# Experts' weight loads: the float64 half piece queued ahead of the step's float32 piece

## The chip, the core and the metric

One core of a Trainium2 chip runs the kernel. The metric is the device time of one execution in microseconds (us). Five engines matter: TensorE (PE, matrix products and transposes; its weight loads are PEld), VectorE (DVE), ScalarE (ACT), GpSimd (POOL) and SyncE (SP), which only starts transfers. Each engine works through its own instructions in order and waits at semaphores for the others. A transfer started by SP, ACT or POOL is carried out by 16 DMA engines beside them.

## What is computed

Three layers follow one another on 1536 tokens of width 512: attention with local and global keys, a mixture of 8 experts of which each token takes 2, and a last dense layer.

```python
x = attention(q, k, v)                      # 2 x 768 tokens, 8 heads of 64
logits = x @ w_gate + log1p(exp(x @ w_noise)) * noise
top2, top2_w = two_largest(logits)          # softmax weights of the two
for e in range(8):                          # tokens that chose expert e
    h = maximum(x[mask] @ w1[e], 0)         # 512 -> 1024
    out[mask] += top2_w[mask] * (h @ w2[e]) # 1024 -> 512
h = out @ w_in                              # 512 -> 2048
y = (h * tanh(softplus(h))) @ w_out         # 2048 -> 512
```

The weights of the experts come as float32, those of the last layer as float64.

## The kernel before

The program has three stages: attention (to about 124 us), the experts (to about 464 us) and the last layer. Every product is made of three: a float32 number is split into a rounded part, `hi`, and the rest, `lo`, and PE adds hi x hi, hi x lo and lo x hi (`three`, L767 to L769).

The experts' stage is a loop over 64 steps. Step n = 8e + f is expert e, slice f. In each step the program writes down, and every engine keeps that order for itself:

- `first_layer(n)`: 12 products into `hp`, then ACT makes `hhi` (L813) and DVE `hlo` (L814);
- in slices 2 to 4 `turn_out`: four transposes of the last expert's result into the one PSUM tile `tq`, a copy to `ys` by ACT (L849), and a store to `yd` on ACT's queue (L850);
- `whole_layer(n - 1)`: 12 products into the four tiles `ac`, with the `hhi` and `hlo` of the step before;
- in slices 3 to 6 of experts 1 to 6 `turn_in`: four transposes (L801) of the next expert's tokens `xg` into the same `tq`, split by ACT (L772) and DVE (L773);
- `w_split`: the float32 piece n + 2 of the experts' weights (128 x 1024, in a tile `raw`) is split, `whi` by ACT (L264) and `wlo` by DVE (L267);
- `w_load`: SP starts the load of piece n + 4 (L252, 512 KB);
- in slices 1, 3 and 5 (in the first expert 3, 5 and 7, at the end also steps 62 and 63) a half piece of the last layer's float64 weights is turned into `whil` and `wlol`: two instructions of DVE make `t` (L300, L301), ACT rounds it (L295), DVE adds four more (L302, L303, L296, L297). L303 is the last that reads the half piece;
- `w64_load`: if the next step converts, SP starts the load of that half piece (L274, 512 KB) into a tile `raw`.

So a half piece is wanted one step after its load and a float32 piece two steps after. Both kinds share three buffers (`wraw`, bufs=3). A new tile takes the buffer that was let go first, and its load waits until the last reader of that buffer is done. SP starts its transfers one after another, each as soon as its own wait has ended.

At the end of the last expert's steps the program gathers rows of the other experts' results for the first tokens (`rest_rows`, L918, on POOL, in step 61), which waits for all their stores; weighs them (L925 on ACT, L926 on DVE, step 63); converts one more half piece; and then turns them on PE (`rest_turn`, L933) among the last products, with copies (L945) and transposes (L952) behind them.

```python
        if n:
            w_split(A, V)
            w_load()
        half = w64_begin() if conv else None
        if half:
            for op in half[:4]:
                op()
            half[4]()
        if n + 1 in CONVS if n < 60 else True:
            w64_load()
```

Of the kernel before, what the change touches and what calls it, by code (L numbers as in the profile page):

```python
# [49 lines left out]
CONVS = [8 * e + f for e in range(8) for f in CONV]  # L50
# [113 lines left out]
def build(tc, ctx, I, out, n_global, n_local, dbg=None):  # L164
# [82 lines left out]
    def w_load():  # L247
        j = state["load"]
        if j < 64:
            state["load"] += 1  # L250
            raws[j] = wraw.tile([P, 1024], F32, name="raw")
            nc.sync.dma_start(raws[j], I["w_moe"][j])  # L252

    def w_split(e_hi, e_lo):
        j = state["split"]
        if j == 64:
            return
        state["split"] += 1
        hi = wring.tile([P, 1024], F32R, name="whi")
        lo = wring.tile([P, 1024], F32R, name="wlo")  # L260
        pieces[j] = (hi, lo)
        raw = raws.pop(j)
        if e_hi is A:
            A.activation(hi, raw, AF.Copy)  # L264
        else:
            e_hi.tensor_copy(hi, raw)
        e_lo.tensor_tensor(lo, raw, hi.bitcast(F32), op=OP.subtract)  # L267

    def w64_load():
        j, s = divmod(state["load64"], 2)  # L270
        if j < 16:
            state["load64"] += 1
            raws[j, s] = wraw.tile([P, 512, 2], I32, name="raw")
            nc.sync.dma_start(raws[j, s], I["w_moe2"][j, :, s * 512:(s + 1) * 512].bitcast(I32)  # L274
                              .rearrange("p (a b) -> p a b", b=2))
# [33 lines left out]
    def gather(e, blocks=NT):  # L309
        for c, n in CHUNKS:  # L310
            k = e * 4 + c // P
            idx = (gidx if blocks == NT else gidx0)[:n, k:k + 1]
            xg = xg_p.tile([P, DM], F32, name="xg")
            G.indirect_dma_start(out=xg[:n], out_offset=None, in_=xd[:1 + blocks * P],  # L314
                                 in_offset=bass.IndirectOffsetOnAxis(ap=idx, axis=0))
            xgs[e, c] = xg
# [477 lines left out]
    def turn_in(e, ci, pool, name):  # L794
        c, n = CHUNKS[ci]
        if ci == 0:
            xgT[e] = parts()
        xg = xgs.pop((e, c))
        tp = pool.tile([P, 4, P], F32, name=name)
        for d in range(4):  # L800
            T.transpose(tp[:, d, :n], xg[:n, d * P:(d + 1) * P], ident[:n, :n])  # L801
        split_ps(xgT[e][0][:, :, c:c + n], xgT[e][1][:, :, c:c + n], tp[:, :, :n])

    def first_layer(e, f):
        whi, wlo = (w.rearrange("p (d f) -> p d f", d=4) for w in pieces[8 * e + f // 2 * 2])
        xhi, xlo = xgT[e]
        c = (f % 2) * P
        hp = ps_h.tile([P, 512], F32, name="hp")
        for d in range(4):
            three(hp[:, :CAP], whi[:, d, c:c + P], wlo[:, d, c:c + P], xhi[:, d], xlo[:, d], d == 0, d == 3)  # L810
        hhi = mk.tile([P, CAP], F32R, name="hhi")
        hlo = mk.tile([P, CAP], F32R, name="hlo")
        A.activation(hhi, hp[:, :CAP], AF.Relu)  # L813
        V.scalar_tensor_tensor(hlo, hp[:, :CAP], 0.0, hhi.bitcast(F32), op0=OP.max, op1=OP.subtract)  # L814
        hT[e, f] = (hhi, hlo)
# [12 lines left out]
    def whole_layer(e, f):  # L828
        for _ in second_layer(e, f):
            pass  # L830
        if f == 7:
            yT[e] = mk.tile([P, 4, CAP], F32, name="yT", bufs=1)
            for d in range(4):
                if d % 2:
                    V.tensor_copy(yT[e][:, d], yps[e][d][:, :CAP])
                else:
                    A.activation(yT[e][:, d], yps[e][d][:, :CAP], AF.Copy)

    def turn_out(e, ci, pool, name):
        c, n = CHUNKS[ci]  # L840
        tp = pool.tile([P, 4, P], F32, name=name)
        for d in range(4):
            T.transpose(tp[:n, d], yT[e][:, d, c:c + n], ident)
        store_y(e, ci, tp)
# [7 lines left out]
    def some_places(t, n, name):  # L852

        ohr, ohc, ops = places_of(t, n, wlast.tile([P, 1024], F32R, name=name).bitcast(F32))
        for op in ops:
            op()
        return ohr, ohc

    def whole_list(parts):
        list_of(parts, ps_q.tile([P, 4, P], F32, name="tq").rearrange("p a b -> p (a b)")[:, :64])  # L860
# [36 lines left out]
    def places():  # L897

        oh = mk.tile([P, DM], F32, name="ys", bufs=3).rearrange("p (t s) -> p t s", s=P)
        for t in range(TC):  # L900
            V.tensor_scalar(oh[:, t], iot[:, :P], chi[:, t:t + 1], None, op0=OP.is_equal)
        ps = ps_q.tile([P, TC + 1, P], F32, name="tq")
        for t in range(TC):
            T.transpose(ps[:, t], oh[:, t], ident)
        for t in range(TC):
            T.matmul(ps[:, TC, :1], oh[:, t], wlh[:, 1, t:t + 1], start=(t == 0), stop=(t == TC - 1))
        V.tensor_copy(place, ps[:, :TC])
        V.tensor_copy(wslot, ps[:, TC, :1])

    def rest_rows():  # L910

        rl, rh = parts()
        got = []
        for t in range(TC):
            r = []
            for k, (w, idx) in enumerate(((rl, cidx[:, 0, t:t + 1]), (rh, crest[:, t:t + 1]))):
                y = w.rearrange("p a b -> p (a b)")[:, t * DM:(t + 1) * DM].bitcast(F32)
                G.indirect_dma_start(out=y, out_offset=None, in_=yd[:(E - 1) * CAP, :],  # L918
                                     in_offset=bass.IndirectOffsetOnAxis(ap=idx, axis=0))
                r.append(y)  # L920
            got.append(r)
        return got

    def rest_sum(t, r):
        A.activation(r[0], r[0], AF.Copy, scale=wlh[:, 0, t:t + 1])  # L925
        V.scalar_tensor_tensor(r[1], r[1], wrest[:, t:t + 1], r[0], op0=OP.mult, op1=OP.add)  # L926
# [80 lines left out]
    for n, (e, f) in enumerate(steps):  # L1007
        if f == 0 and 0 < e < E - 1:
            gather(e + 1)
        first_layer(e, f)  # L1010
        if early and n < len(PARTS):
            lists.append(some_places(*PARTS[n]))
        if n == 1 and not early:
            gather(1)
        if 2 <= f <= 4 and e:
            turn_out(e - 1, f - 1, ps_q, "tq")
        if n == 7:
            turn_in(1, 3, ps_q, "tq")
        if n:
            whole_layer(*steps[n - 1])  # L1020
        if f == 1 and e:
            turn_out(e - 1, 0, ps_q, "tq")
        if n == LISTS and early:
            whole_list(lists)
            gather(1)
        if n == WEIGH[0]:
            weigh()
        if n == WEIGH[1]:
            places()
        if (e, f) == (E - 1, 5):  # L1030
            rest = rest_rows()
        if (e, f) == (E - 1, 7):
            for t in range(TC):
                rest_sum(t, rest[t])
        for ci in range(3 if e == 0 else 4):
            if f == (TURN if e == 0 else (3, 4, 5, 6))[ci] and e + 1 < E:
                turn_in(e + 1, ci, ps_q, "tq")
        conv = n in CONVS if n < 61 else True
        if n:
            w_split(A, V)  # L1040
            w_load()
        half = w64_begin() if conv else None
        if half:
            for op in half[:4]:
                op()
            half[4]()
        if n + 1 in CONVS if n < 60 else True:
            w64_load()
    late = finish(rest)
    if "y" in dbg:  # L1050
        nc.sync.dma_start(dbg["y"], yd[:7 * CAP])
# [257 lines left out]
```

## Time and profile before

| what | value |
|---|---|
| median of 3 runs | 764.21 us (762.32 to 766.95) |
| the profiled execution | 765.73 us |
| its span, first to last instruction | 763.9 us |
| PE busy | 724.5 us (95%) |
| DVE busy | 601.4 us (79%) |
| ACT busy | 384.9 us (50%) |
| POOL busy | 162.8 us (21%) |
| transfers | 89.28 MB, 117 GB/s over the span |
| mean granted TensorE clock | 0.991 |

The span is the time from the first to the last instruction of one execution that the hardware profiler followed. "Idle before" an instruction is time in which its engine did nothing, with the event that ended the wait. A DMA's time in the chain of waits runs from its start on the queue until the engine that wanted the data could go on. An engine's pause costs the kernel only where no other engine's work covers it, so a wait of DVE is of interest where one of PE follows from it.

### The profile page before, as it was taken

Reading aid. Unit: us, or ns where it says so; the run is one execution under the profiler, and the core shown is the slowest. Engines: PE = TensorE matmul, PEld = TensorE weight load, DVE = VectorE, ACT = ScalarE, POOL = GpSimd, SP = SyncE. Lnnn points to the kernel's source line nnn. Section 1 sums busy time; section 2 is a strip of 40 time slices with the busy share of each in tenths; the row PEclk is TensorE's granted clock in tenths of the full one; section 3 lists DMA queues with packets and bytes.
Section 4 is the critical chain, followed back from the end, with each engine's and each line's share of the span. In section 5 each row is a group of like instructions: output and inputs, shape, how many; then the busy total and the mean of one; then the engine's idle time right before and its main releaser. Section 6 shows DMA issues by size and latency. Waiting matters only on the chain.

```text
span 763.9 us, 11872 instructions
## 1 busy us (share of the span) xinstructions
PE 724.5 (95%) x4257; PEld 636.3 (83%) x4257; DVE 601.4 (79%) x1297; ACT 384.9 (50%) x814; POOL 162.8 (21%) x167
## 2 busy tenths in 40 slices
PE   8999989999999999999999999888899999999995
PEld 4665669899998989899999987766789898989894
DVE  7677767986768575757676597999999999999985
ACT  5787742344444444444444446444555555555453
POOL 2012030210101020101100031555333424432221
PEclk9999989999999999999999999999999999999999
DMA  6677421556655564646554552311020111101001
GB/s 173 201 190 183 141 76 44 169 194 195 189 168 190 166 193 152 210 155 214 165 183 139 179 196 79 105 55 28 1 69 29 29 42 27 32 26 42 1 0 46
DMA packets 42935, 89.28 MB, mean 117 GB/s; under 512 B 5987, under 2 KB 18403, under 8 KB 42868
## 3 DMA queue, kind: packets, MB, share of 16 engines
q1 hardware_dynamic: 35412, 69.37, 29.4%
q0 software_dynamic: 4096, 13.11, 5.8%
q10 hardware_dynamic: 3360, 5.97, 2.1%
q8 instruction: 35, 0.57, 0.3%
q14 instruction: 32, 0.26, 0.1%
HBM read 75.32 MB, written 13.11 MB: 116 GB/s over the span
## 4 chain that ended last, share of the span: by engine, by line
PE 64%; DVE 18%; ACT 6%; DMA 6%; issue 4%; POOL 1%; ACTq 1%; POOLq 0%; DVEq 0%
PE hp L767 8%; PE hp L768 8%; PE hp L769 8%; DMA raw<-in_w_moe 5%; PE ac L1133 4%; PE ac L1134 4%; PE ac L1138 4%; PE sp L485 4%; PE ac L767 4%; PE ac L769 4%; PE ac L768 4%; PE xp L530 3%; PE tp L516 3%; DVE wlo L267 3%; DVE yT L1090 2%
## 5 line engine op out<-in xcount | busy, mean ns | idle before, releaser
L1106 POOL TENSOR_TENSOR yT<-yT 128x384 f32<-128x384 f32 (+1 forms) x68 | 71.5, 1051 | 191.0 <-DVE yT L1105 173.3
L767 PE MATMUL hp<-xgh,whi 128*128 128x416 f32 (+1 forms) x288 | 104.3, 362 | 0.0
L267 DVE TENSOR_TENSOR wlo<-raw,whi 128x1024 fp32r<-128x1024 f32 x61 | 74.6, 1223 | 34.8 <-ACT whi L264 34.1
L769 PE MATMUL hp<-xgh,wlo 128*128 128x416 f32 (+1 forms) x288 | 100.8, 350 | 0.0
L768 PE MATMUL hp<-xgl,whi 128*128 128x416 f32 (+1 forms) x288 | 100.7, 350 | 0.0
L767 PE MATMUL ac<-hhi,whi 128*128 128x416 f32 x256 | 91.7, 358 | 0.0
L768 PE MATMUL ac<-hlo,whi 128*128 128x416 f32 x256 | 90.0, 352 | 1.5 <-DVE hlo L814 1.5
L769 PE MATMUL ac<-hhi,wlo 128*128 128x416 f32 x256 | 89.8, 351 | 0.0
L1109 ACT ACTIVATE hhi<-yT 128x384 fp32r<-128x384 f32 (+1 forms) x68 | 34.4, 506 | 93.8 <-POOL yT L1106 93.8
L314 POOL DMA_INDIRECT xg<-xd,gidx x32 | 32.2, 1005 | 219.7 <-PE tq L801 196.9
L767 PE MATMUL hp<-xgh,whil 128*128 128x384 f32 x224 | 76.4, 341 | 0.0
L768 PE MATMUL hp<-xgl,whil 128*128 128x384 f32 x224 | 75.7, 338 | 0.5 <-DVE xgl L773 0.5
L769 PE MATMUL hp<-xgh,wlol 128*128 128x384 f32 x224 | 75.3, 336 | 0.0
L264 ACT ACTIVATE whi<-raw 128x1024 fp32r<-128x1024 f32 x64 | 67.5, 1054 | 8.5 <-ACT ys L849 6.9
L1090 DVE SCALAR_TENSOR_TENSOR yT<-yT 128x384 f32<-128x384 f32 (+1 forms) x68 | 63.2, 929 | 2.3
L1133 PE MATMUL ac<-whil,hhi 128*128 128x512 f32 x144 | 58.2, 404 | 2.1 <-ACT hhi L1109 2.0
L813 ACT ACTIVATE hhi<-hp 128x416 fp32r<-128x416 f32 x64 | 32.6, 510 | 49.0 <-PE hp L769 46.7
L1134 PE MATMUL ac<-wlol,hhi 128*128 128x512 f32 x144 | 56.6, 393 | 0.0
L768 PEld LDWEIGHTS hp<-xgl,whi 128*128 128x128 f32 x288 | 54.3, 189 | 0.9 <-DVE xgl L670 0.3
L767 PEld LDWEIGHTS hp<-xgh,whi 128*128 128x128 f32 x288 | 54.1, 188 | 0.8
L769 PEld LDWEIGHTS hp<-xgh,wlo 128*128 128x128 f32 x288 | 54.0, 188 | 0.5
L295 ACT ACTIVATE whil<-t 128x512 fp32r<-128x512 f32 x26 | 16.4, 633 | 73.5 <-DVE t L301 65.9
(241 smaller groups left out, 1625.4 us busy)
## 6 DMA issues: line engine op xcount, KB each, us to landing
raw<-in_w_moe SPq DMA_DIRECT2D x96, 512.0 KB
yd<-ys ACTq DMA_DIRECT2D x21, 256.0 KB
ks<-in_k_t SPq DMA_DIRECT2D x24, 136.0 KB
qr<-in_q_t SPq DMA_DIRECT2D x24, 128.0 KB
vt<-in_v_w SPq DMA_DIRECT2D x12, 256.0 KB
xd<-xs SPq DMA_DIRECT2D x12, 256.0 KB
out<-ys SPq DMA_DIRECT2D x12, 256.0 KB
vt<-in_v_w SPq DMA_DIRECT2D x10, 208.0 KB
```

The source lines that it names most:

```text
L264: A.activation(hi, raw, AF.Copy)
L267: e_lo.tensor_tensor(lo, raw, hi.bitcast(F32), op=OP.subtract)
L314: G.indirect_dma_start(out=xg[:n], out_offset=None, in_=xd[:1 + blocks * P], in_offset=bass.IndirectOffsetOnAxis(ap=idx, axis=0))
L767: T.matmul(ps, whi, xhi, start=first, stop=False)
L768: T.matmul(ps, whi, xlo, start=False, stop=False)
L769: T.matmul(ps, wlo, xhi, start=False, stop=last)
L813: A.activation(hhi, hp[:, :CAP], AF.Relu)
L1090: V.scalar_tensor_tensor(t, v, 2.0, v, op0=OP.add, op1=OP.mult)
L1106: G.tensor_tensor(v, v, t, op=OP.mult)
L1109: A.activation(g[0][:, cc], m[1][:, cc], AF.Copy)
L1133: T.matmul(acc2[tb][c], ghi[:, cc], whi, start=(f == 0), stop=False)
L1134: T.matmul(acc2[tb][c], ghi[:, cc], wlo, start=False, stop=False)
```

## The change

The block that starts the load of the float64 half piece moves from the end of the step to the place ahead of `w_split` and `w_load`. In the 23 steps that load both kinds (slices 0, 2 and 4; in the first expert 2, 4 and 6; not step 60, where no float32 piece is left) the half piece now stands ahead of the piece in SP's queue. No instruction is added or removed, none changes its size, and POOL computes in these steps neither before nor after.

```diff
         conv = n in CONVS if n < 61 else True
+
+        if n + 1 in CONVS if n < 60 else True:
+            w64_load()
         if n:
             w_split(A, V)
             w_load()
         half = w64_begin() if conv else None
         if half:
             for op in half[:4]:
                 op()
             half[4]()
-        if n + 1 in CONVS if n < 60 else True:
-            w64_load()
```

SP's queue in expert 2, slices 0 to 4, before. L252 loads a float32 piece, L274 a half piece; the numbers behind `raw` only tell tiles apart.

```order
L252 DMA raw_2850<-in_w_moe 128x1024
L274 DMA raw_2852<-in_w_moe2 128x1024
L252 DMA raw_2899<-in_w_moe 128x1024
L252 DMA raw_2953<-in_w_moe 128x1024
L274 DMA raw_2955<-in_w_moe2 128x1024
L252 DMA raw_3007<-in_w_moe 128x1024
L252 DMA raw_3066<-in_w_moe 128x1024
L274 DMA raw_3068<-in_w_moe2 128x1024
```

Of each pair with a half piece the float32 piece stands first. The same eight places of SP's queue in the changed program:

```order
L274 DMA raw_2846<-in_w_moe2 128x1024
L252 DMA raw_2852<-in_w_moe 128x1024
L252 DMA raw_2899<-in_w_moe 128x1024
L274 DMA raw_2949<-in_w_moe2 128x1024
L252 DMA raw_2955<-in_w_moe 128x1024
L252 DMA raw_3007<-in_w_moe 128x1024
L274 DMA raw_3062<-in_w_moe2 128x1024
L252 DMA raw_3068<-in_w_moe 128x1024
```

In slices 0, 2 and 4 the two loads have changed places; in slices 1 and 3 there is one load, where it was. In the built program every one of these places has the same wait on DVE as before: in slice 2 the first place waits for L303 of slice 1 and the second for L267 of slice 2, whichever load stands there. The instructions of PE, DVE, ACT and POOL stand in the same order as before.

SP's queue in the last expert, slices 2 to 7, before:

```order
L252 DMA raw_4919<-in_w_moe 128x1024
L274 DMA raw_4921<-in_w_moe2 128x1024
L252 DMA raw_4964<-in_w_moe 128x1024
L274 DMA raw_5018<-in_w_moe2 128x1024
L274 DMA raw_5070<-in_w_moe2 128x1024
```

And in the changed program:

```order
L274 DMA raw_4915<-in_w_moe2 128x1024
L252 DMA raw_4921<-in_w_moe 128x1024
L252 DMA raw_4964<-in_w_moe 128x1024
L274 DMA raw_5014<-in_w_moe2 128x1024
L274 DMA raw_5057<-in_w_moe2 128x1024
```

Only slice 2 has two loads to exchange; behind it no float32 piece is left to stand beside a half piece.

## Rows read from the trace of the kernel before

**Rows 1.** Page, part 1: engine, busy us, share of the span, instructions.
```profile
PE 724.5 (95%) x4257; PEld 636.3 (83%) x4257; DVE 601.4 (79%) x1297; ACT 384.9 (50%) x814; POOL 162.8 (21%) x167
```
**Rows 2.** Waits: engine, line, whom it waited for, us in total, times, longest.
```profile
DVE t L300 <- DMA raw<-in_w_moe: 6.0, 7, 2.6
...
PE tq L801 <- ACT ys L849: 7.2, 6, 1.6
```
**Rows 3.** Timeline, DVE, expert 2: start, us, instruction, idle before and what ended it.
```profile
221.11 0.69 DVE L303 SCALAR_TENSOR_TENSOR wlol<-raw,t 128x512 fp32r<-128x512 uint32 x1
...
228.20 1.22 DVE L267 TENSOR_TENSOR wlo<-raw,whi 128x1024 fp32r<-128x1024 f32 x1 [0.26 <-ACT whi L264]
229.92 0.43 DVE L300 TENSOR_SCALAR t<-raw 128x512 int32<-128x512 int32 x1 [0.50 <-DMA raw<-in_w_moe]
...
239.91 1.23 DVE L267 TENSOR_TENSOR wlo<-raw,whi 128x1024 fp32r<-128x1024 f32 x1 [0.26 <-ACT whi L264]
241.05 0.42 DVE L300 TENSOR_SCALAR t<-raw 128x512 int32<-128x512 int32 x1
```
**Rows 4.** Timeline, ACT and then PE, expert 2, slice 4.
```profile
232.04 0.57 ACT L849 ACTIVATE ys<-tq 32x512 f32<-32x512 f32 x1
...
232.66 0.66 PE L801 MATMUL tq<-ident,xg 128*128 128x128 f32 x4 [1.14 <-ACT ys L849]
```
**Rows 5.** Timeline, SP's queue: starts in expert 2, slices 2 and 4.
```profile
221.83 0.33 SPq L252 DMA_DIRECT2D raw<-in_w_moe  x1
224.98 0.33 SPq L274 DMA_DIRECT2D raw<-in_w_moe  x1
...
236.18 0.33 SPq L274 DMA_DIRECT2D raw<-in_w_moe  x1
```
**Rows 6.** Chain of waits: start, us, what; two half piece loads.
```profile
152.46 4.03 DMA raw<-in_w_moe
...
266.27 5.33 DMA raw<-in_w_moe
```
**Rows 7.** Timeline, ACT: a store beside the loads, and where pieces are wanted.
```profile
222.21 0.33 ACTq L850 DMA_DIRECT2D yd<-ys  x1
...
233.85 1.05 ACT L264 ACTIVATE whi<-raw 128x1024 fp32r<-128x1024 f32 x1
...
243.44 1.05 ACT L264 ACTIVATE whi<-raw 128x1024 fp32r<-128x1024 f32 x1
```
**Rows 8.** Timeline, SP, DVE and ACT, expert 7, slices 2 to 4.
```profile
428.57 0.33 SPq L252 DMA_DIRECT2D raw<-in_w_moe  x1
...
432.82 1.23 DVE L267 TENSOR_TENSOR wlo<-raw,whi 128x1024 fp32r<-128x1024 f32 x1 [0.63 <-ACT whi L264]
436.63 0.43 DVE L300 TENSOR_SCALAR t<-raw 128x512 int32<-128x512 int32 x1 [2.59 <-DMA raw<-in_w_moe]
...
439.79 1.06 ACT L264 ACTIVATE whi<-raw 128x1024 fp32r<-128x1024 f32 x1 [0.46 <-ACT ys L849]
```
**Rows 9.** Timeline, PE, end of expert 7: its three pauses.
```profile
440.86 0.46 PE L768 MATMUL ac<-hlo,whi 128*128 128x416 f32 x1 [0.55 <-DVE hlo L814]
455.49 1.83 PE L933 MATMUL hp<-ident,xgl 128*128 128x128 f32 x14 [0.85 <-DVE xgl L926]
459.27 0.33 PE L952 MATMUL ac<-ident,yT 128*128 128x128 f32 x1 [1.17 <-DVE yT L945]
```
**Rows 10.** Chain of waits, expert 7: loads, store and gather, in order of time.
```profile
431.71 4.90 DMA raw<-in_w_moe
...
439.36 3.50 DMA yd<-ys
...
449.11 4.80 DMA xgh<-yd,cidx
```
**Rows 11.** Timeline, DVE, end of expert 7.
```profile
453.34 0.75 DVE L926 SCALAR_TENSOR_TENSOR xgl<-xgl,wrest,xgh 128x512 f32<-128x512 f32 x1 [0.56 <-ACT xgh L925]
454.68 0.75 DVE L926 SCALAR_TENSOR_TENSOR xgl<-xgl,wrest,xgh 128x512 f32<-128x512 f32 x1 [0.58 <-ACT xgh L925]
```

## The prediction

> **What bounds the kernel now.** I read the page's busy shares first, then who waited for whom, then the timeline of one expert. PE is busy 95% of the span [rows 1], so only what makes PE pause, or ends one of its pauses sooner, moves the time. In the experts' stage the waits name one pause that comes again: PE's transposes of `turn_in` (L801) wait six times, 7.2 us in all, for ACT's copy L849 [rows 2], which frees the one tile `tq`. The timeline of expert 2 shows why the copy is late. In slice 3 DVE ends the split L267 at 228.20 + 1.22 = 229.42, then has nothing to do for 0.50 us until a half piece has landed, and starts L300 at 229.92 [rows 3]. ACT rounds that half piece before it comes to the copy, and works in order; so the copy starts at 232.04 and PE's transposes, after a pause of 1.14 us, at 232.66 [rows 4]. The half piece that is waited for was started at 224.98, at the second place of slice 2, while the first place of that slice started a float32 piece at 221.83 [rows 5]. So a load is waited for once in each of seven experts: seven waits of DVE, 6.0 us in all, the longest 2.6 [rows 2]. The longest is that of expert 7 [rows 8]; the other six, in experts 1 to 6, are 6.0 - 2.59 = 3.4 us, and each stands ahead of one of PE's six pauses. Those are 7.2 - 3.4 = 3.8 us longer than the waits, 0.63 us each: the part that is DVE's and ACT's own work.
>
> **The change, part by part.** Nothing is added or taken away. In 23 steps the two loads of a step exchange their places in SP's queue, and with them their buffers and waits; the instants at which SP can start, and the bytes, stay. Two things are left to price.
>
> *The half piece starts sooner.* In slice 2 of expert 2 it gets the place of 221.83 in place of 224.98, 3.15 us sooner [rows 5]; that place opens when L303 has read the half piece before, at 221.11 + 0.69 = 221.80 [rows 3]. What it needs is to be in by 229.42. The trace has no landing time for the load that stands at this place now, so I bound it: the half piece loads that the chain shows take 4.03 us (first expert, with no store of results beside it) to 5.33 us (the longest) [rows 6]. At 5.33 it lands at 227.16, 2.3 us before DVE wants it; at 4.03 sooner still. The wait goes whole. What is late next is DVE itself: without a wait L300 starts 0.09 us before the end of L267 (239.91 + 1.23 = 241.14 against 241.05 [rows 3]), so each wait that goes gives 0.09 us more than it is long. For experts 1 to 6 that is 3.4 + 6 x 0.09 = 3.9 us. The copy L849 comes as much sooner and PE's pause shrinks by as much, to some 0.55 us; it cannot give more than the wait, since the chain from the split through L300, L301, ACT and L849 keeps its length. Behind the pause PE has no other wait until the next expert, so the gain is kept. I take 3.9 us; the lower end is zero (next part), the upper 3.9.
>
> *Expert 7.* There is no `turn_in`, so the half piece is wanted sooner: the split ends at 432.82 + 1.23 = 434.05 and L300 waits until 436.63 [rows 8]. From the first place, at 428.57 [rows 8], the longest of the loads lands at 428.57 + 5.33 = 433.90, just in time; with the 4.90 us that this one took [rows 10] at 433.5. So DVE's work there starts 2.59 + 0.09 = 2.7 us sooner. How much of it reaches PE is the uncertain term. PE has three pauses behind it: 0.55 us (for `hlo`, itself behind the conversion), 0.85 us (for L926) and 1.17 us (for the copy L945, which stands behind the last conversion on DVE) [rows 9], 2.6 us together, which is the upper bound. The lower bound is the first alone, 0.55 us. Between them: the last store of expert 6's results starts behind the same conversion, at 439.36, lands in 3.50 us, and only then POOL gathers; the last gather's data are in at 453.9 [rows 10]. All of that moves by 2.7 us, and then DVE's two idle pieces between the L926, 0.56 and 0.58 us [rows 11], have no cause left. DVE ahead of them is nearly full but waits for PE's first layers, which move only by the 0.55 us of the first pause. So the last conversion comes at least 0.55 + 0.56 + 0.58 = 1.7 us sooner, at most 2.6. I take 2.0 us.
>
> *The float32 piece starts later.* It gets the second place and must pay for nothing as long as it lands before ACT's `whi` two steps on. In slice 2 of expert 2 the second place starts at 224.98 [rows 5] and `whi` at 233.85 [rows 7], 0.6 us sooner after the change: 8.3 us. In slice 4 it is 236.18 [rows 5] to 243.44 [rows 7], 7.3 us. In expert 7, slice 2, it is 431.71 [rows 10] to 439.79 [rows 8], and this `whi` comes 2.7 us sooner: 5.4 us. The longest load takes 5.33 us [rows 6], and the load at that very place 4.90 us [rows 10]. So the cover holds everywhere, with 2 us to spare in experts 1 to 6 and hardly any in expert 7, where being late by some tenths would cost tenths of the 2.0 us. I set this at zero.
>
> A rule speaks against the first of these. The load at the earlier place has a store of results beside it, started on ACT's queue at 222.21 [rows 7]. The Trainium skill (DMA: Bandwidth & Descriptors, Queues, rings and completion order) says that each DMA engine takes turns, packet by packet, among the queues that have work for it. The trace agrees as far as it goes: 4.03 us without a store, 4.9 to 5.3 us beside stores. By the rule an earlier start could lose to the store what it gains; by the rows the loss is at most 5.33 - 4.03 = 1.3 us of the 3.15, and the sum stays. As a forecast of its own it is the second rival below.
>
> The sum is 3.9 + 2.0 = 5.9 us. The profiled execution took 765.73 us with a span of 763.9; by the sum they would be 759.8 and 758.0. It stood 1.5 us above the median of the runs, 764.21; against the median I predict 758.3 us, 0.8% less.
>
> **The rivals.**
>
> *Expert 7 gives almost nothing.* If the gathers, or the float32 piece that has hardly any slack there, hold DVE back, only the pause of 0.55 us goes: 3.9 + 0.55 = 4.5 us, 759.8 us. For it: DVE waits for PE's first layers at the end; against it: two idle pieces of DVE and three pauses of PE hang on the same late half piece.
>
> *The earlier place is no earlier.* The load there has the store beside it; if that stretched it to 229.92 - 221.83 = 8.1 us, the wait would stay. The gain would be nothing, 764.2 us, or in part up to 1 us. Against it: no load in the chain took more than 5.33 us [rows 6].
>
> *More than the pauses.* If the residual 0.55 us of the six pauses also shrank and expert 7 gave its 2.6 us, the gain would be 3.9 + 3.3 + 2.6 = 9.8 us at most; some 8 us, 756.2 us, if half of the first did. Against it: that residue is the length of the chain behind L267, which stays.
>
> *Slower: the float32 piece is late.* ACT works in order, and a `whi` that waits holds the `hhi` behind it and so PE. It decides from 7.3 us of landing on in slice 4 and 8.3 us in slice 2; to eat the 5.9 us gained in seven experts, slice 4's load would have to take 7.3 + 0.85 = 8.1 us in each. At 10 us the loss is (2.7 + 1.7) x 7 = 31 us against 5.9 gained: 789 us. The rows hold nothing over 5.33 us.
>
> **How the numbers follow.** Forecast (gain 5 to 7 us) 0.65; expert 7 gives nothing 0.15; the earlier place no earlier 0.10; more 0.06; slower 0.04. A measurement of this kernel can tell about 0.5%, 3.8 us, from no change. The three runs of before lie 4.6 us apart, so a median may be off by 1.5 us. The forecast's own range is 757 to 759.5 us, with that 755.8 to 760.8. Its upper end is drawn to 762.0 us to take in the first rival whole and a part of the second; beyond it lie most of the second rival and the slower case, below it half of the case of more: under 2 in 10. Faster by over 0.5%: nearly all of the forecast and of the case of more, and two thirds of the first rival, 0.60 + 0.06 + 0.10 = 0.76. Within 0.5%: the rest of these and the second rival, 0.20. Slower: 0.04.
>
> **What would show it.** In the new profile DVE's waits for a load ahead of L300 should be gone or under 0.5 us in all; PE's waits for L849 should fall from 7.2 to about 3.3 us in six pauses of 0.55; the pauses of 0.55 and 0.85 us in expert 7 should be gone and that of 1.17 us smaller. In SP's queue L274 should start in the places where L252 did. I am wrong if ACT's `whi` waits for a load, if DVE still waits ahead of L300, or if the pauses shrink and the experts' stage is as long as before.

## The result and the profile after

The changed kernel takes 760.98 us (median of 20 runs), the kernel before 769.26 us in its 20 runs beside it (the first three of them are those of the table, with 764.21 us; most of the others lay higher). The ratio is 0.990, with a 95% interval of 0.988 to 0.993: 1.0% faster, or 7.5 us of 764, with 5.7 to 9.3 us open. The forecast was 758.3 us, 0.8% or 5.9 us less; that gain lies inside the interval. The profiled execution took 760.73 us; its span is 758.9 us.

First the page of the changed kernel, part 1 (busy us, share, instructions):

```profile
PE 726.1 (96%) x4257; PEld 638.8 (84%) x4257; DVE 601.4 (79%) x1297; ACT 384.9 (51%) x814; POOL 163.0 (21%) x167
```

The instructions are the same in number, and the busy times of DVE, ACT and POOL hardly differ from [rows 1]. PE's is 1.6 us longer, all of it outside the experts, while the span is 5.0 us shorter. The waits (us in total, times, longest) have one line left of the two of [rows 2]:

```profile
PE tq L801 <- ACT ys L849: 3.3, 6, 0.6
```

No wait of DVE for a load is left in the experts. The timeline of the changed kernel at the place of [rows 3 to 5], expert 2, SP's queue, DVE and PE:

```profile
221.92 0.33 SPq L274 DMA_DIRECT2D raw<-in_w_moe  x1
...
225.06 0.33 SPq L252 DMA_DIRECT2D raw<-in_w_moe  x1
...
228.27 1.23 DVE L267 TENSOR_TENSOR wlo<-raw,whi 128x1024 fp32r<-128x1024 f32 x1 [0.26 <-ACT whi L264]
229.41 0.42 DVE L300 TENSOR_SCALAR t<-raw 128x512 int32<-128x512 int32 x1
...
232.15 0.66 PE L801 MATMUL tq<-ident,xg 128*128 128x128 f32 x4 [0.56 <-ACT ys L849]
```

The half piece (L274) stands at the first place of the slice, the float32 piece (L252) 3.1 us behind it. L300 starts 0.09 us before the split ends, and PE's pause has gone from 1.14 to 0.56 us.

Whole executions also differ in the attention stage, which the change does not touch, so I read the experts' stage by itself: from the first start of L769 on `xgh` to the first start of L961. These two rows (ns shortest, median, longest; then first and last start in us) of the kernel before and then of the changed one:

```profile
L769 PE MATMUL hp<-xgh,wlo x288: 334/353/358, 124.8 to 748.4; 128*128 128x416 f32 x128, 128*128 128x384 f32 x16
...
L961 PE MATMUL hp<-place,raw x6: 333/381/446, 461.1 to 462.5; 128*128 128x384 f32 x6
```

```profile
L769 PE MATMUL hp<-xgh,wlo x288: 333/353/353, 125.9 to 743.3; 128*128 128x416 f32 x128, 128*128 128x384 f32 x16
...
L961 PE MATMUL hp<-place,raw x6: 333/381/440, 456.1 to 457.4; 128*128 128x384 f32 x6
```

The stage was 461.1 - 124.8 = 336.3 us long and is 456.1 - 125.9 = 330.2 us: 6.1 us less, against 5.9 forecast. The whole span shows only 5.0 us of it, because attention took 1.1 us longer in the second execution. PE's busy time in the stage is 324.35 us before and 323.73 us after.

### The profile page after: what moved, and what is told of

Read it like the earlier page. It is cut to its first block, busy times and chain, and to the rows that moved or that the text cites. A ratio compares the mean times of both kernels' runs of the same rounds, so it can differ in the third digit from the quotient of the medians.

```text
span 758.9 us, 11879 instructions
## 1 busy us (share of the span) xinstructions
PE 726.1 (96%) x4257; PEld 638.8 (84%) x4257; DVE 601.4 (79%) x1297; ACT 384.9 (51%) x814; POOL 163.0 (21%) x167
## 4 chain that ended last, share of the span: by engine, by line
PE 73%; DVE 16%; ACT 4%; issue 4%; DMA 1%; POOL 1%; ACTq 0%; POOLq 0%; DVEq 0%
PE hp L767 9%; PE hp L768 9%; PE hp L769 9%; PE ac L768 5%; PE ac L767 5%; PE ac L769 5%; PE ac L1134 4%; PE ac L1135 4%; PE ac L1139 4%; PE sp L485 4%; PE xp L530 3%; PE tp L516 3%; DVE yT L1091 2%; PE tq L801 2%; DVE wlo L267 2%
## 5 line engine op out<-in xcount | busy, mean ns | idle before, releaser
L267 DVE TENSOR_TENSOR wlo<-raw,whi 128x1024 fp32r<-128x1024 f32 x61 | 74.6, 1224 | 35.7 <-ACT whi L264 35.1
L769 PE MATMUL hp<-xgh,wlo 128*128 128x416 f32 (+1 forms) x288 | 100.7, 350 | 0.0
L769 PE MATMUL ac<-hhi,wlo 128*128 128x416 f32 x256 | 89.9, 351 | 0.0
L314 POOL DMA_INDIRECT xg<-xd,gidx x32 | 32.5, 1016 | 215.6 <-PE tq L801 192.8
L769 PE MATMUL hp<-xgh,wlol 128*128 128x384 f32 x224 | 75.3, 336 | 0.0
L769 PEld LDWEIGHTS hp<-xgh,wlo 128*128 128x128 f32 x288 | 54.0, 188 | 0.4
L814 DVE SCALAR_TENSOR_TENSOR hlo<-hp,hhi 128x416 fp32r<-128x416 f32 x64 | 37.5, 586 | 19.2 <-ACT hhi L813 19.0
```

What stands on the lines that cost most here:

```text
L769: T.matmul(ps, wlo, xhi, start=False, stop=last)
```

## The experiments

Theory: what counts is that the half piece of slice 2 has landed when DVE wants it in slice 3; its lateness reaches PE through ACT's rounding, which stands ahead of the copy that frees `tq`. Rivals: the order of the loads matters everywhere; the lateness goes by another way; expert 7 gives nothing. The length of the experts' stage is taken from the same two rows in every profile.

| kernel | ratio to before (95% interval) | experts' stage, us | DVE's six waits + expert 7, us |
|---|---|---|---|
| before | 1 | 336.3 | 3.4 + 2.6 |
| before, once more | | 339.6 | 3.9 + 3.7 |
| the change | 0.990 (0.988 to 0.993) | 330.2 | 0 + 0 |
| the change, once more | 0.988 (0.982 to 0.993) | 330.7 | 0 + 0 |
| exchange in experts 1 to 6, slice 2 | 0.995 (0.991 to 0.998) | 333.8 | 0 + 3.2 |
| exchange in expert 7, slice 2 | 0.998 (0.995 to 1.001) | 337.9 | 4.6 + 0 |
| exchange elsewhere | 0.996 (0.993 to 0.9995) | 339.5 | 3.7 + 3.8 |
| exchange elsewhere, once more | 0.999 (0.996 to 1.003) | 337.5 | 4.3 + 2.6 |
| stores later, order of before | 0.995 (0.992 to 0.998) | 334.5 | 0.3 + 2.8 |
| half piece one slice later | 1.050 (1.043 to 1.056) | 374.6 | 27.1 + 2.7 |
| rounding later, order of before | 0.988 (0.983 to 0.993) | 330.1 | 3.3 + 3.7 |
| rounding later and the change | 0.986 (0.981 to 0.990) | 325.4 | 0 + 0 |
| all roundings later and the change | 0.978 (0.972 to 0.983) | 324.5 | 0 + 0 |

### The parts of the change one by one

The exchange is made under a condition, and left as before elsewhere:

```diff
         conv = n in CONVS if n < 61 else True
+        ahead = f == 2 and 1 <= e <= 6
+        if ahead and (n + 1 in CONVS if n < 60 else True):
+            w64_load()
...
-        if n + 1 in CONVS if n < 60 else True:
+        if not ahead and (n + 1 in CONVS if n < 60 else True):
             w64_load()
```

> The exchange of the two loads in slice 2 of experts 1 to 6 alone; everywhere else the order of before. Theory (what counts is that the half piece of slice 2 lands before DVE wants it): DVE's six waits of 0.2 to 0.9 us go, PE's six pauses fall to 0.55 us each, expert 7 keeps its wait of about 2.6 us and its pauses; 4.0 us less than before (0.5%), about 1.8 us more than with the whole change. Rival (the order matters in every step, by the spread of the traffic): a share of 6 in 23 of the measured 7.5 us, 2 us. Rival (the waits are longer in most executions than in the one that was profiled): 5 to 6 us.

Measured: 0.54% less (0.22% to 0.87%), 4.1 us. DVE's waits in experts 1 to 6 are gone, that in expert 7 stays (3.17 us there), and PE's six pauses are 3.3 us together, as with the whole change. The interval parts the expected 4.0 us neither from a share of 2 us nor from 5 to 6; that the six waits and pauses are what went, the traces show.

With the condition `(e, f) == (7, 2)`:

> The exchange in slice 2 of expert 7 alone. Theory: the six pauses of PE stay as before (0.86 to 1.55 us), DVE's wait of 2.6 us in expert 7 goes, PE's pauses of 0.55 and 0.85 us there go and that of 1.17 us stays; 1.8 us less than before (0.2%). Rival (expert 7 gives almost nothing): 0.5 us or less.

Measured: 0.2% less (from 0.5% less to 0.1% more), 1.5 us. The six pauses stay, 8.4 us together, and the wait of expert 7 is gone with PE's first pause behind it. Its second pause, which I had expected gone as well, is 0.62 us here. The interval does not part 1.8 us from 0.5; the traces do: from the last of the six pauses to the pause for L945 it is 402.04 to 461.94, 59.9 us, where the kernel before took 61.1 (its rows stand below, with the account of expert 7).

With the condition `not (f == 2 and e)`, twice:

> The exchange everywhere but in slice 2 of experts 1 to 7: slices 0 and 4 and the first expert. Theory: no wait hangs on these loads, at most 0.3 us less than before, in the first expert. Rival (the order matters in every step): 16 in 23 of the measured 7.5 us, 5 us less.

> The exchange everywhere but in slice 2 of experts 1 to 7, once more, since its first interval left 0.05% to 0.7% open. Theory (only the first expert gains): 0.3 to 0.8 us less than before, an interval that holds 0.1%. Rival (the loads of slices 0 and 4 count as well): 2.9 us less again, 0.4%.

Measured: 0.38% less (0.05% to 0.72%) and then 0.08% less (0.45% less to 0.28% more). The first does not hold the theory's 0.3 us, the second does. In both profiles the waits and pauses of slice 3 stand as before, and what is shorter is the one pause of the first expert for `xgl`: 0.28 and 0.31 us in place of 0.61 and 0.78 in the two of before. The traces show nothing that the order in slices 0 and 4 costs; the two times together, about 0.2% less, are hardly clear of nothing.

### The way from the load to PE

ACT's rounding of the half piece of slice 3 is written down behind the copy of the next step, in experts 1 to 6; the exchange is not made:

```diff
             for op in half[:4]:
                 op()
-            half[4]()
+            if f == 3 and 1 <= e <= 6:
+                round_later = half[4]
+            else:
+                half[4]()
...
             turn_out(e - 1, f - 1, ps_q, "tq")
+            if f == 4 and round_later:
+                round_later()
+                round_later = None
```

> The order of the loads as before; only ACT's rounding of the half piece of slice 3, with DVE's two instructions behind it, is written down one step later in experts 1 to 6. Theory (the late half piece reaches PE through ACT's order alone: the rounding stands ahead of the copy that frees tq): DVE still waits 0.2 to 2.4 us ahead of L300, but the six pauses of PE go whole, 7.2 us less than before or a little more (1%), and expert 7 keeps its wait and pauses. Rival (it reaches PE through DVE's order, by hlo and xgl behind the conversion): pauses of 0.5 us and more stay, 3.3 us less than before.

Measured: 1.2% less (0.7% to 1.7%). DVE's waits in experts 1 to 6 are still there, 3.3 us together (one of them, 1.1 us, in slice 5). Its timeline, DVE and PE in expert 3, shows the wait without the pause:

```profile
267.28 0.43 DVE L300 TENSOR_SCALAR t<-raw 128x512 int32<-128x512 int32 x1 [1.47 <-DMA raw<-in_w_moe]
```

```profile
267.75 0.60 PE L801 MATMUL tq<-ident,xg 128*128 128x128 f32 x4
```

DVE waits 1.47 us for the half piece and PE's transposes start without a pause. The longest of its pauses in experts 1 to 6 is one of 0.59 us, in expert 3 as well, behind an `hlo`: it follows the wait of 1.1 us in slice 5. So the lateness of slice 3 reached PE through ACT's order; the way through DVE's order exists too, and in expert 7, whose pauses are for `hlo` and L926, it is the only one seen. The same with the exchange:

> The whole change, and in experts 1 to 6 ACT's rounding of the half piece of slice 3 with DVE's two instructions behind it is written down one step later, behind ACT's copy of the results. Theory (the 0.55 us that each pause of PE keeps is the chain from the split through L300, L301 and ACT to the copy): the six pauses go, 3.3 us less than with the change alone. Rival (something else holds the copy or the transposes, the tile of xg or the products): the pauses stay at 0.3 to 0.55 us and the time is that of the change.

Measured: 1.45% less (1.0% to 1.9%); the six pauses are gone altogether, and the stage is 325.4 us, 4.8 us under that of the change alone. That is more than the 3.3 us of the pauses themselves. The other 1.5 us stand in PE's busy time, 322.33 us in the stage against 323.73 with the change alone: 1.4 us less, 0.23 us for each pause that went whole. In which products this lies I have not settled.

> The whole change, with ACT's rounding written down one step later in every step that converts before step 60. Theory (in the experts 1 to 6 the chain counts in slice 3 alone; in the first expert a pause of 0.95 us for hlo stands behind a conversion, and in expert 7 the copy behind the late half piece comes sooner): up to 1.5 us less than with the later rounding in slice 3 alone, 1.5% to 1.7% less than before. Rival (moved work only lands elsewhere): as with slice 3 alone, 1.45%, or worse.

Measured: 2.2% less (1.7% to 2.8%), the fastest of all. The stage is 324.5 us: only 0.9 us less than with slice 3 alone, of which the pause of 0.95 us in the first expert is the visible part. The rest of the distance between 1.45% and 2.2% stands in no row of the experts, and most of it is not the kernel's: five of these six runs had a mean granted clock of 0.992 or more, and two of the six with slice 3 alone. At 0.994 to 0.997 the runs here took 750.2 to 752.4 us, those with slice 3 alone 752.6 and 752.7, and the kernel before, run in the same series as those here, 763.4 to 765.5; by these the gain is about 1.7%.

### A dose the other way

```diff
             w_load()
+        if f == 3 and 1 <= e <= 6:
+            w64_load()
         half = w64_begin() if conv else None
...
-        if n + 1 in CONVS if n < 60 else True:
+        if (n + 1 in CONVS if n < 60 else True) and not (f == 2 and 1 <= e <= 6):
             w64_load()
```

> The order of before, but in slice 2 of experts 1 to 6 the half piece is not loaded; it is loaded in slice 3, behind that step's float32 piece. A dose the other way. Theory (PE's pause follows the landing one for one): the half piece starts at the end of DVE's split and lands 3.5 to 4 us later, so DVE's six waits are 3.5 to 4 us in place of 0.6, PE's six pauses about 4.2 us in place of 1.2, and the time 18 us above before. Rival (something covers a longer wait in part): pauses of PE shorter than DVE's waits, under 10 us.

Measured: 5.0% more (4.3% to 5.6%), 38 us, where I had expected 18. The waits are somewhat longer than expected, but the pauses do not account for it. Waits of that kernel, and its timeline, DVE and PE in expert 2:

```profile
PE tq L801 <- ACT ys L849: 31.0, 6, 5.5
DVE t L300 <- DMA raw<-in_w_moe: 30.3, 8, 4.8
```

```profile
242.56 0.43 DVE L300 TENSOR_SCALAR t<-raw 128x512 int32<-128x512 int32 x1 [4.61 <-DMA raw<-in_w_moe]
```

```profile
245.31 1.12 PE L801 MATMUL tq<-ident,xg 128*128 128x128 f32 x4 [5.25 <-ACT ys L849]
...
246.92 0.55 PE L769 MATMUL hp<-xgh,wlo 128*128 128x416 f32 x1
```

Wait and pause still go one for one: 4.61 and 5.25, again 0.64 apart. But behind the pause four transposes take 1.12 us where they took 0.66 [rows 4], and a product 0.55 us where the median is 0.35. The stretches of the same kernel tell why (columns: stretch, its length, busy us of each engine with its instructions, granted clock, DMA share, GB/s):

```profile
240.00:245.30 5.30, 0.06 (x1) 0.00 (x0) 2.63 (x5) 1.50 (x3) 0.00 (x0) 0.83 0.16 54
245.30:249.00 3.70, 3.69 (x13) 3.56 (x14) 3.06 (x5) 1.54 (x2) 0.94 (x1) 0.50 0.66 197
249.00:253.00 4.00, 4.00 (x22) 3.89 (x20) 0.85 (x2) 0.52 (x1) 0.00 (x0) 0.84 0.48 162
253.00:257.00 4.00, 4.00 (x24) 3.96 (x22) 2.82 (x4) 1.55 (x2) 0.94 (x1) 1.00 0.24 66
```

After the pause PE is granted half the clock (1.2 of 2.4 GHz) for 3.7 us and 0.84 of it in the next 4 us. In work lost that is 3.7 x 0.5 + 4 x 0.16 = 2.5 us behind this pause, and 15 us if each of the six cost as much; with the 31.0 - 7.2 = 23.8 us that the pauses are longer, 38.8 us, against the 374.6 - 336.3 = 38.3 us by which the stage grew. PE's busy time says nearly the same: 338.29 us in the stage against 324.35, 13.9 us more. The Trainium skill (TensorE: Matmul & The Clock Gate, HAM oscillation) describes a kernel whose products wait for a load again and again and start at the lower clock each time. The trace agrees for this pause, with 0.50; shorter ones, below, did not all lower it.

### Why the load took so long, and how it varies

In the order of before, two stores of results that ACT starts beside the half piece's load are started in slice 5:

```diff
         A.activation(ys[:n], tp[:n].rearrange("p a b -> p (a b)"), AF.Copy)
+        if ci in (1, 2) and e < 6:
+            stores.append((yd[e * CAP + c:e * CAP + c + n, :], ys[:n]))
+            return
...
+        while f == 5 and stores:
+            nc.scalar.dma_start(*stores.pop(0))
         if n:
             w_split(A, V)
```

> The order of the loads as before; in experts 1 to 6 the two stores of results that stand on ACT's queue in slices 2 and 3, beside the half piece's load, are started in slice 5. Theory (the load takes 4.6 to 5.3 us because these stores share the DMA engines with it): it lands in about 4 us, DVE's six waits go or fall under 0.2 us and PE's pauses to about 0.6 us, 3.5 to 4.5 us less than before (0.5%). Rival (the load takes that long for itself, or because of the float32 piece ahead of it): waits and time as before.

Measured: 0.49% less (0.16% to 0.82%), 3.7 us. Its waits, and its half piece in expert 2 (SP, then DVE):

```profile
PE tq L802 <- ACT ys L850: 3.7, 6, 0.9
DVE t L300 <- DMA raw<-in_w_moe: 3.1, 2, 2.8
```

```profile
227.46 0.33 SPq L274 DMA_DIRECT2D raw<-in_w_moe  x1
...
232.01 0.42 DVE L300 TENSOR_SCALAR t<-raw 128x512 int32<-128x512 int32 x1
```

Started at the old, late place, the half piece is in when DVE comes to it, under 4.6 us after its start; one wait of 0.3 us is left in experts 1 to 6 (in expert 3, behind a load of 4.9 us) and that of expert 7, whose stores were not moved. So the late place alone does not make the wait: in five of six experts the stores beside it were needed.

The stores may not be the only transfer that counts. In the kernel that loads the half piece one slice later no store stands beside it, but in experts 1 to 5 a gather of POOL (L314) that was started 2.6 us ahead. Its loads in experts 5 and 6, the second without a gather (chain of waits):

```profile
381.23 4.70 DMA raw<-in_w_moe
...
428.99 3.60 DMA raw<-in_w_moe
```

With the gather they took 4.52 to 4.80 us, without it 3.60. In the order of before that gather starts 1.9 us behind the load, and expert 6, which has none, shows no shorter load there (4.92 us in the first profile). It was not moved, so its part stays open.

Nor is the early place only a head start. In the changed kernel the same two stores are started 0.4 and 2.8 us behind the half piece, not 2.8 and 0.4 us ahead of it, and its landings that the traces hold (experts 2 and 4) came 4.0 us after the start, in the second profile 4.3 and 4.4. The load itself is shorter there than nearly all at the late place, which took 4.5 to 6.8 us (one was in within 4.4).

The kernel before once more:

> The kernel before once more, to see how its waits for the half piece vary from one execution to the next. Theory (the profiled execution of before had waits near the short end): DVE's six waits in experts 1 to 6 together 3.4 to 5 us, that of expert 7 2.6 to 3.8 us. Rival (the waits are the same in every execution): 3.4 and 2.6 us.

Measured: six waits of 3.9 us together, 3.7 us in expert 7. From the chain of waits of this execution, two half piece loads of slice 2 (start, us, what):

```profile
222.45 5.12 DMA raw<-in_w_moe
...
263.95 5.76 DMA raw<-in_w_moe
```

The longest in experts 1 to 6 is now 5.76 us, where the longest in [rows 6] took 5.33 (that of expert 7 took 5.96, where it had been 4.90); the wait behind the load of 5.76 us is 1.33 us and PE's pause 1.98 us. Four stretches around that pause:

```profile
262.00:269.60 7.60, 7.60 (x48) 7.34 (x47) 4.25 (x6) 3.10 (x5) 0.96 (x1) 1.00 0.80 245
269.60:272.50 2.90, 0.92 (x6) 0.58 (x4) 2.67 (x5) 1.50 (x3) 0.00 (x0) 1.00 0.47 167
272.50:276.00 3.50, 3.50 (x14) 3.37 (x15) 3.19 (x5) 1.54 (x2) 0.94 (x1) 0.61 0.76 215
276.00:280.00 4.00, 4.00 (x23) 3.89 (x22) 0.59 (x1) 0.83 (x2) 0.07 (x1) 0.91 0.45 158
```

Behind the 2.0 us the clock fell too: 3.5 x 0.39 + 4 x 0.09 = 1.7 us of work lost. In the profile that I predicted from, the longest pause was 1.55 us, and the stretch behind it was run at full clock:

```profile
274.40:278.00 3.60, 3.60 (x21) 3.57 (x22) 3.29 (x6) 2.07 (x3) 0.94 (x1) 1.00 0.78 229
```

Two more of the profiles above have a long pause in expert 3: 3.05 us in the kernel with the exchange in expert 7 alone, 2.83 us in the first with the exchange elsewhere. The clock of the next 3.5 us was 0.57 and 0.58. PE's busy time in the stage parts the five profiles with the order of before in experts 1 to 6: 324.3 and 324.4 us where no pause was over 1.70 us and the clock stayed up, 325.3 to 326.2 in the three with a fall.

The loads of over 5.5 us are all those of two experts, 3 and 7. In the kernel with the exchange in expert 7 alone, the load of expert 3 (chain of waits) and one line of the DMA queues while it ran:

```profile
266.97 6.83 DMA raw<-in_w_moe
```

```profile
q8 instruction: 1, 0.02, 0.9%
```

One transfer of this queue, of the kind `instruction`, falls into the late load of experts 3 and 7 in every profile with the order of before in slice 2, and into that of no other expert. The long loads, 5.8 to 6.8 us, are all among these, though others among them took 4.9 to 5.5. In the changed kernel the early load of these experts is over 4.6 us old when it comes. Whether this transfer stretches the load was not tried.

The changed kernel once more:

> The changed kernel once more. Theory (its half pieces are in before they are wanted in every execution): no wait of DVE ahead of L300 in the experts, six pauses of PE at 0.55 us, the experts' stage 330.7 us long as in its first profile, where two profiles of the order of before have 336.9 and 340.2; 0.7% to 1.2% less than before. Rival (the changed kernel has executions with waits too): single waits of 0.3 us or more, a stage of 332 us or more.

Measured: 1.2% less (0.7% to 1.8%). Its profiled execution spent 132.7 us in attention, against 125.9, so only the experts are read: no wait of DVE, six pauses of 3.3 us together, a stage of 330.7 us, 0.5 from that of the first profile. (The stages named in the expectation were read to a later row, 0.5 to 0.6 us longer than in the table.) In expert 7 one pause of 0.65 us for L926 is left, which the first profile did not have. The four profiles with the order of before in slice 2 of all seven experts have 336.3, 339.6, 339.5 and 337.5 us.

## Why the prediction was right, and where it was not

*The half piece starts sooner.* Right in its mechanism and in its size for the execution it was made from: DVE's six waits are gone, PE's six pauses fell from 7.2 to 3.3 us, 3.9 us as summed, and the residue is 0.55 us each, as put down from the 0.09 us of overlap. That this residue is the chain from the split to the copy was shown by writing the rounding down later: the pauses vanish. The step "it cannot give more than the wait" held in that execution, whose longest pause was 1.55 us; behind the 1.98 us of the other it would not have. It also leaves out what a pause costs when it goes whole: by the later rounding, about 0.23 us of PE's busy time beside its length.

*Expert 7.* I took 2.0 us between 0.55 and 2.6; from the last of the six pauses to the pause for L945 the shift grew from 398.14 - 394.88 = 3.26 to 459.27 - 454.20 = 5.07 us, so the expert gave 1.8 us. Where that stretch begins, PE before and then after:

```profile
398.14 0.66 PE L801 MATMUL tq<-ident,xg 128*128 128x128 f32 x4 [1.13 <-ACT ys L849]
```

```profile
394.88 0.66 PE L801 MATMUL tq<-ident,xg 128*128 128x128 f32 x4 [0.55 <-ACT ys L849]
```

The waits that make the term came out otherwise. Rows of the changed kernel, DVE, ACT and PE:

```profile
430.72 0.42 DVE L300 TENSOR_SCALAR t<-raw 128x512 int32<-128x512 int32 x1
```

```profile
434.42 1.06 ACT L264 ACTIVATE whi<-raw 128x1024 fp32r<-128x1024 f32 x1 [1.02 <-PE ac L768]
436.90 0.52 ACT L813 ACTIVATE hhi<-hp 128x416 fp32r<-128x416 f32 x1 [1.42 <-PE hp L769]
```

```profile
454.20 0.33 PE L952 MATMUL ac<-ident,yT 128*128 128x128 f32 x1 [1.17 <-DVE yT L945]
```

L300 starts 5.91 us sooner than in [rows 8], 2.65 us of it gained in this expert, as forecast. Then ACT has to wait 1.02 us with the next `whi` and 1.42 us with the next `hhi`, both times for PE's products: here PE is the bound, as I had said of the first layers, and I had not seen that `whi` waits for products as well. The pauses of 0.55 and 0.85 us [rows 9] are gone, 1.4 of the 1.8 us; the rest is PE's busy time in this stretch, 58.55 us before and 58.08 after. That of 1.17 us is unchanged, where I had expected it smaller: it reads 1.17 or 1.18 us in every profile. The size that I took is near by some luck, since it stands on one pair. In the five profiles with the late half piece in expert 7 and the stores and roundings in place, the stretch takes 61.1 to 62.6 us, in the three with the exchange there 59.3 to 59.9; its gain is 1.2 to 3.3 us by the pair, 2.3 us between the means. So the rival that expert 7 gives almost nothing fell. The upper end of 2.6 us was not a bound: a longer wait has more to give.

*The float32 piece starts later.* No `whi` waits for a load in either profile of the changed kernel: the cover holds. In expert 7 that was partly luck. The float32 piece of slice 2 landed 4.9 us after its start in the first profile and 5.4 in the second, as much as the whole cover that I had reckoned, 5.4 us; ACT was held about 1.0 us by PE's products at that place and did not come to it sooner. How late the piece could come was not tried.

*The first expert*, at which I put nothing, gives 0.3 us: its pause of 0.61 us is 0.32.

*The earlier place is no earlier* fell: no wait is left. At the early place, with both stores started behind it, the half piece took 4.0 to 4.4 us, not the 8.1 of this rival. What the stores cost at the late place is shown by moving them: without them the load is in time in five of six experts. The Trainium skill (DMA: Bandwidth & Descriptors, Queues, rings and completion order) has each DMA engine take turns among the queues with work; the runs agree in that a load beside the stores of another queue comes later than one without them, and do not show in what turns.

*The sum.* The experts' stage gave 6.1 us in the profiled pair; 5.9 was forecast. The runs say 7.5 us (5.7 to 9.3), which still holds 5.9, so the runs alone do not show that the sum is short; the profiles do. The time itself, 760.98 us, came out 2.7 above the forecast, because the kernel before lay 5 us higher in this series than in the three runs that I subtracted from, and the larger gain took back part of that. What I mis-sized is the step that takes the durations from one execution: the wait for a load is not a fixed cost. In five profiles with the order of before it came to 3.4 to 4.6 us in experts 1 to 6, and in five to 2.6 to 3.8 us in expert 7, and the one that I read from had the least of both. A long one among them costs PE's clock besides, as in three of the five. My reading of the loads was narrow as well: one beside stores took 4.64 us in the same chain, and other executions have 6.8. The stage of 336.3 us that I started from is the shortest of four, and against the others, 337.5 to 339.6, the change gives 7.3 to 9.4 us. So a forecast nearer 7 us was to be had only from several executions.

## What to carry to other kernels

Two loads that take turns in a queue are worth ordering by when they are wanted, not by the order of the program's own parts: one was wanted a step later and the other two, and their exchange, with the same starts and the same waits at each place, cost nothing that the traces show. Where a late load hurts through an engine's order, as ACT's rounding ahead of a copy here, writing the copy down first gave about as much as the earlier load (0.988 against 0.990), and both together more (325.4 us of stage against 330.1 and 330.2). A wait for a transfer in one profile is a sample: look at it in several executions before it becomes a term of a sum.

## What I had not expected of the hardware

The same 512 KB load of expert 3, slice 2, with the same stores beside it, took 5.33 us in one execution, 5.76 in the next and up to 6.83 in others; started some 3 us sooner, ahead of the stores, the loads of experts 2 and 4, whose landings the traces hold, took 4.0 to 4.4 us. And some pauses of PE cost more than their length: behind 1.55 and 1.70 us the granted clock stayed 1.00, behind 1.98, 2.83 and 3.05 us it was 0.57 to 0.61 over 3.5 us and behind 5.25 us 0.50 over 3.7 us, which in the kernel with the late half piece made about 14 of the 38 us lost.
